# Decay attention with a gated convolution: the turns cut into 64-row halves, the states into column halves, and each copy given an engine of its own

## The chip, the cores and the metric

The kernel runs on one core of a Trainium2 chip, as one launch. The metric is the device time of that core in microseconds (us); lower is better. TensorE (PE in the profile) multiplies, VectorE (DVE) and ScalarE (ACT) work element by element, GpSimd (POOL) copies and issues some transfers, SyncE (SP) issues the other transfers. Results of PE land in PSUM, eight banks, from where DVE or ACT must copy them into SBUF before PE can use them again.

## What is computed

All data are 32-bit floats. For each of 4 batches and 8 heads (768 steps, 48 wide) a complex state of 48 x 48 decays by a per-step factor and takes in an outer product:

```
scale = min(|a|, 0.999) / (|a| + 1e-6);  a = (a_re + i a_im) * scale
S = a[t] * S + outer(k[t], v[t])          # S complex, k and v real
y[t] = q[t] @ real(S)
```

Then y is laid out as x (batch, 768, 384) and goes through a gated layer:

```
gate = sigmoid(sum over 5 taps of conv_w[tap] * x shifted by the tap)
out  = (gate * (x @ w_val)) @ w_out
```

## The kernel before

**The attention.** The products of the decays are written as exp and cos/sin of running sums, so that a head's step t has a key row `kx` and a query row `qx` of 96 numbers (cosine and sine part). The work is cut into nine units (a batch, its heads, a half of its steps; the first unit has two heads, the second six, the other seven eight). For each unit ACT computes logarithms, arctangent, sines and exponentials, DVE the products and running sums between them (`p_ln` to `p_query`, letters a to r of the order), and DVE ends with `kx` and then `qx` (L477).

**Turns.** `kx` and `qx` have steps on the partitions; scores need them with the 96 numbers on the partitions. `flips` (letter T, L526) turns them on PE: three multiplications by the identity per head and half, 128 steps each, into one PSUM bank (`mm`, four of them). `flip_copies` (U) copies the bank into `kT` or `qT`.

**Scores, states, outputs.** Per chunk of 128 steps and pair of heads: `scores` (s, L555 to L560) multiplies kT by qT, in four pieces that lie in the upper or lower 64 partitions of a bank; `masks` (M, L571) multiplies the bank by the causal mask on DVE; `states` (t, L593) adds kn^T v of a chunk to the running state, 96 rows high, in the bank `S_ps`; `state_copies` (u) copies it into `S_sb` or `S_cr`; `outputs` (y, L628 to L638) adds the state's part and the chunk's own part; `output_copies` (v) copies the result into `y_sb`. A multiplication of 32-bit numbers leaves two records of the profile, a turn one. `kn` is `kx` with other steps on the partitions: it is stored to DRAM (`store_kd`, K) and loaded back (`load_kn`, N).

**The layer.** `collects` (X) moves `y_sb` into `xT` by transfers on POOL's queue. `conv` (C and D) runs five taps per 128 channels, the first as a scaled copy on ACT (L147), the other four on DVE (L691). `gates` (G) is the sigmoid on ACT, `values` (P, L722) and `projects` (O, L729) the two multiplications, `gateds` (Z, L746) the product with the gate on DVE, `row_copies` (Q) and `stores` (W) the way out.

**Order.** Every step is a letter, and the string `ORDER` lists all steps once. Instructions are emitted in that order, and `turn` pins each engine's instructions, and SP's and POOL's transfers, to the order of emission. So each engine has one fixed queue, and an instruction that waits holds everything behind it on its engine. Copies out of PSUM are all made by `act_copy` (L149), on ACT.

Of the kernel before, what the change touches and what calls it, by code (L numbers as in the profile page):

```python
# [25 lines left out]
BUFS = {'in': 4, 'v': 2, 'kn': 2, 'xT': 2, 'z': 2, 'lv': 2, 'an': 2, 'tmp': 2, 'qx': 2, 'kx': 1, 'kT': 6, 'S': 1, 'S_sb': 3, 'S_cr': 4, 'y_sb': 3, 'sm': 2, 'ot': 2, 'mm': 4, 'y': 1}  # L26
# [3 lines left out]
TAP0 = 'act'  # L30
ORDER = (
    "AAVLaaAbcceafgadiibclmhhdcwjwwwhhjwkknpewpBfkkwwoVgqArowqriinooTTBAaAaUAlmpbUpTUqATUrKcdqTUTLwssANtr"
    "TaTTuAhMMyhacUjwUUbsvceyvkcMskseBfnKtugfMigTdiyvtuilwooilshympAAANtmvMuTThqUUqtujUUtuprMTrUTTtyTuVUU"
    "UTTTvysMpkUtvTpsMkUsTautaUyuAbUMTvTKUAqUAcywTTvyNcUUsesUMMsrvTntfXXyoouwvgUTMdTtyUUXvTTiUXutqBUAhATr"
    "AhiATwauyUwLUalmpjtsskTTpTvMMbUUsUywcMvkTTcUUwTUyvTXTunTewyUTTqUsTUUwvosoMsyrMwMXvXKNtuATTUfUyvqgBUX"
    "UrPituTXCDDTTtyUUKUuNasMstTTaUiulvDsUyCmXCMTCMtCvCCDPputypGZCUDACvuPtdhTTuhtUTUTCGybUUssjutPvkwXMysk"
    "wPGcuZZZdhtTMMnovoyTUTTZAAqOcrvyqhQXeUTTUTUTUTXXUTUUUTjvUsfAAsrMyaMsvkayMPukvyVOnboBvgcWZKUoNiilmXXX"
    "DXtDuTDCCCOUtQDWTTTDQTAAutUTUUUssDDUcOMWDDupTpMOOrtQTWQTyCCqGWUvsAQDuydMvTUUtuUTTTAAtUqKrhPhGGPyeaUU"
    "sTvjNaZTUMyfubZcgBkPPPkZviiltZXZVmssMydnooTAXpTMTutvyBchqWUTUTUTUTeUUUUTTTUfqOKsspMgMiivysvyhutQUUTr"
    "TTvUMTUlmuAyUUvssMyMrvpsMyvTTjUTTpUUUXXNtuXXkkTTTUtUunPZotuTTqTyBUUUssMMTToTvysvyqUUArrKNUUtuTUTTtuO"  # L40
    "vQXMyUUsvsMyMvsMyvTTtuTTUUUtuUTTtUTTTutUyUUssUXvCDMyvMsyCXCCuvTUMTTCCUUTUtWWPTTTUCyuCUUssXMMvyvCDDDD"
    "CsMyEPvOOQQXWWXOQWGZXXPPPGZGZZZPtODCOOuCDDDDDCCQWDDDDCZQWQWyGvXOQWPZGEEGOQWOQWOCQPPZDCZOOCCCGDQDDDWG"
    "QWXCCPZPPCCCGOZZOOOQWQWWQQWW"
# [9 lines left out]
def kernel(  # L53
# [12 lines left out]
    nc = tc.nc  # L66
# [82 lines left out]
    def act_copy(out, in_):  # L149
        return turn("act", nc.scalar.copy(out, in_))  # L150
# [141 lines left out]
    def weights():  # L292
        cw_row = const.tile([TAPS * NT, P], F32, name="cw_row")
# [91 lines left out]
    def p_sec(u):  # L385
        tf, tj = rate(u, "tmp", "tmp")
        act(tf, views(u, "an")[0], AF.Square)
        yield
        act(tf, tf, AF.Ln, bias=1.0, sets=[LE])
        yield  # L390
# [127 lines left out]
    def flips():  # L518
        for u, (b, h0, g, f0, nf) in enumerate(units):
            for rs, (s, nm) in [(rs, x) for rs in groups[u] for x in ((0, "kx"), (1, "qx"))]:  # L520
                src = tl[u][nm].rearrange("p (j f h) c d -> p j f h (c d)", f=nf, h=g)
                for f in range(nf):
                    for h in [r + w * (g // 2) for r in rs for w in range(2)]:
                        pt = mm().rearrange("p (j x) -> p j x", j=4)
                        for j in range(JH):
                            pe(nc.tensor.transpose(pt[:C2, j, :], src[:, j, f, h, :], ident))  # L526
                        pts.append((u, s, f0 + f, h, pt))
                        yield

    def flip_copies():  # L530
        while True:
            u, s, f, h, pt = pts.pop(0)
            t = sb.tile([C2, HS], F32, name=("kT", "qT")[s], bufs=BUFS["kT"])
            act_copy(t.rearrange("c (p j) -> c p j", j=JH), pt[:C2, :JH].rearrange("c j p -> c p j"))
            tl[u]["T", s, f, h] = t
            yield
# [44 lines left out]
    def states():  # L581
        for i, (u, n, rs) in enumerate(chunks):
            b, h0, g, f0, nf = units[u]
            if n == NCH - 1:
                continue
            if i == firsts[bank(u, rs)]:
                S_ps[bank(u, rs)] = ps.tile([P, 512], F32, name="S_ps", bufs=BUFS["S"])
            kn = tl[u]["kn", n // HN]
            for r in rs:
                for w in range(2):  # L590
                    h = r + w * (g // 2)
                    at = ((n % HN) * g + h) * C2
                    pe(nc.tensor.matmul(  # L593
                        S_ps[bank(u, rs)][:C2, (2 * (h0 + r) + w) * D:(2 * (h0 + r) + w + 1) * D], kn[:, at:at + C2],
                        v_b[b][:, head(u, h), n],
                        start=(i == firsts[bank(u, rs)] and r == rs[0] and w == 0), stop=(n == NCH - 2),
                        skip_group_check=True,
                    ))
            yield

    def state_copies():
        for u, n, rs in chunks:
# [5 lines left out]
            act_copy(t, S_ps[bank(u, rs)][:C2, 2 * (h0 + rs[0]) * D:2 * (h0 + rs[-1] + 1) * D])  # L608
# [74 lines left out]
    def conv(xT, t0, n, c, z):  # L683
        x0, w0 = xT[:, c, EXT + t0:EXT + t0 + n], cw_sb[:, TAPS - 1, c:c + 1]
        if TAP0 == "act":
            act(z, x0, AF.Copy, scale=w0)
        else:
            dve(nc.vector.tensor_scalar_mul(z, x0, w0))
# [11 lines left out]
    def convs(side):  # L700
        for b, t0, n, c in cspans[side::2]:
# [4 lines left out]
            yield from conv(xTs[b], t0, n, c, zs[b, t0][:, c])  # L706
# [118 lines left out]
    def step_by_step():  # L825
# [7 lines left out]
        with ExitStack() as es:  # L833
# [13 lines left out]
            with tc.For_i(0, S, TB) as t0:  # L847
                tl = {}
                for nm, src in (("ar", a_re), ("ai", a_im), ("k", k), ("q", q), ("v", v)):
# [56 lines left out]
                for b in range(B):  # L906
                    nc.sync.dma_start(
                        out=xd[b, ds(t0, TB), :].rearrange("t (h e) -> h t e", e=D), in_=yo[b * H:(b + 1) * H]
                    )
            with tc.For_i(0, B, 1) as b:  # L910
                xn = sp.tile([P, J, DM], F32, name="xn")
                nc.sync.dma_start(out=xn, in_=xd[ds(b, 1)].rearrange("o (p j) c -> (o p) j c", j=J))
# [13 lines left out]
                for t0 in (0, HS):  # L926
# [5 lines left out]
                    for m in range(t0, t0 + HS, P):  # L932
# [4 lines left out]
                        nc.sync.dma_start(out=out[ds(b, 1), m:m + P].rearrange("o p c -> (o p) c"), in_=ot)  # L937
# [32 lines left out]
```

## Time and profile before

| what | value |
|---|---|
| median of 3 runs | 320.6 us (316.15 to 323.51) |
| the profiled execution, its own time | 317.13 us |
| its span, first to last instruction | 315.4 us |
| PE busy | 275.7 us, 87% |
| DVE busy | 240.7 us, 76% |
| ACT busy | 239.1 us, 76% |
| POOL busy | 63.4 us, 20% |
| granted TensorE clock, mean | 0.982 |

The busy time of PE is the union of its modelled intervals: records of multiplications overlap, so the distance from one start to the next tells what one costs, not its own length. DVE and ACT work on one instruction at a time, and their busy time is work. The 40 slices of the page show where each engine is full: a 9 means at least 90%.

### The profile page before, as it was taken

Reading aid. Unit: us, or ns where it says so; the run is one execution under the profiler, and the core shown is the slowest. Engines: PE = TensorE matmul, PEld = TensorE weight load, DVE = VectorE, ACT = ScalarE, POOL = GpSimd, SP = SyncE. Lnnn points to the kernel's source line nnn. Section 1 sums busy time; section 2 is a strip of 40 time slices with the busy share of each in tenths; the row PEclk is TensorE's granted clock in tenths of the full one; section 3 lists DMA queues with packets and bytes.
Section 4 is the critical chain, followed back from the end, with each engine's and each line's share of the span. In section 5 each row is a group of like instructions: output and inputs, shape, how many; then the busy total and the mean of one; then the engine's idle time right before and its main releaser. Section 6 shows DMA issues by size and latency. Waiting matters only on the chain.

```text
span 315.4 us, 7175 instructions
## 1 busy us (share of the span) xinstructions
PE 275.7 (87%) x2887; PEld 211.5 (67%) x2887; DVE 240.7 (76%) x289; ACT 239.1 (76%) x429; POOL 63.4 (20%) x124
## 2 busy tenths in 40 slices
PE   0342959987899999999999999999998999999992
PEld 0121646876687888787778668898898875655551
DVE  4978989997999999999799996983823692281730
ACT  6999989998899999999999899579445515333211
POOL 6410001132017000643400302331333020030000
PEclk9999987997999999999999999999999999999999
DMA  7999999699579498998269698792582012042111
GB/s 185 197 261 316 331 208 172 216 267 279 147 253 224 181 237 214 194 226 240 57 191 271 238 211 146 239 231 60 188 189 72 22 38 77 0 137 76 52 48 58
DMA packets 73748, 54.80 MB, mean 174 GB/s; under 512 B 28511, under 2 KB 70766, under 8 KB 72814
## 3 DMA queue, kind: packets, MB, share of 16 engines
q1 hardware_dynamic: 71150, 49.57, 62.1%
q0 software_dynamic: 2560, 4.72, 6.2%
q8 instruction: 24, 0.39, 0.5%
q14 instruction: 14, 0.11, 0.1%
HBM read 35.40 MB, written 14.16 MB: 157 GB/s over the span
## 4 chain that ended last, share of the span: by engine, by line
PE 58%; ACT 17%; DVE 10%; DMA 9%; issue 2%; SPq 1%; POOL 0%; DVEq 0%; ACTq 0%; POOLq 0%
PE mm L722 14%; PE mm L729 14%; PE mm L526 8%; PE S_ps L593 5%; DMA kn<-kd 5%; PE y_ps L628 4%; DMA kd<-kx 3%; PE sc_ps L555 3%; DVE kx L477 3%; ACT tmp L147 3%; ACT L145 3%; ACT qx L147 2%; PE y_ps L633 2%; PE y_ps L638 2%; ACT lv L147 2%
## 5 line engine op out<-in xcount | busy, mean ns | idle before, releaser
L157 POOL DMA_DIRECT2D xT<-y_sb x80 | 40.3, 510 | 148.3 <-ACT y_sb L150 115.6
L691 DVE SCALAR_TENSOR_TENSOR z<-xT,cw_sb,z 128x768 f32<-128x768 f32 (+1 forms) x60 | 50.4, 862 | 8.3 <-ACT z L147 6.7
L722 PE MATMUL mm<-xT,w_sb 128*128 128x384 f32 x144 | 49.9, 493 | 0.0
L729 PE MATMUL mm<-w_sb,z 128*128 128x384 f32 x144 | 49.2, 491 | 0.0
L571 DVE TENSOR_TENSOR sm<-sc_ps,mask 128x384 f32<-128x384 f32 (+1 forms) x51 | 26.5, 527 | 19.4 <-PE sc_ps L560 16.7
L593 PEld LDWEIGHTS S_ps<-v_in,kn 128*96 128x96 f32 x320 | 33.3, 170 | 9.9 <-issue 5.3
L593 PE MATMUL S_ps<-v_in,kn 128*96 128x48 f32 x320 | 35.1, 251 | 4.2 <-DMA kn<-kd 3.2
L729 PEld LDWEIGHTS mm<-w_sb,z 128*128 128x128 f32 x144 | 26.6, 190 | 16.8
L722 PEld LDWEIGHTS mm<-xT,w_sb 128*128 128x128 f32 x144 | 26.5, 190 | 16.6
L526 PE MATMUL mm<-ident,kx 128*96 128x128 f32 x192 | 30.3, 293 | 8.0 <-DVE kx L477 8.0
L556 PE MATMUL sc_ps<-qT,kT 96*64 96x128 f32 x192 | 37.0, 289 | 0.0
L555 PE MATMUL sc_ps<-qT,kT 96*64 96x128 f32 x192 | 36.5, 287 | 0.5 <-DVE sm L571 0.5
L150 ACT COPY qT<-mm 96x384 f32<-96x384 f32 x64 | 27.8, 494 | 5.4 <-PE y_ps L628 3.0
L145 ACT ACT_TABLE_LOAD x24 | 30.8, 1283 | 1.2 <-PEq L954 0.8
L150 ACT COPY y_sb<-y_ps 112x256 f32<-112x256 f32 (+1 forms) x51 | 18.7, 367 | 16.0 <-PE y_ps L638 15.8
L526 PEld LDWEIGHTS mm<-ident,kx 128*96 128x96 f32 x192 | 21.7, 136 | 11.3 <-issue 9.1
L150 ACT COPY kT<-mm 96x384 f32<-96x384 f32 x64 | 28.8, 487 | 0.3
L526 PE MATMUL mm<-ident,qx 128*96 128x128 f32 x192 | 28.0, 285 | 0.5 <-DVE lv L443 0.5
L557 PE MATMUL sc_ps<-qT,kT 96*64 96x64 f32 x192 | 27.5, 226 | 0.0
L150 ACT COPY ot<-mm 128x384 f32<-128x384 f32 x24 | 11.1, 475 | 21.6 <-PE mm L729 14.6
L560 PE MATMUL sc_ps<-qT,kT 96*64 96x64 f32 x192 | 27.4, 225 | 0.0
L746 DVE TENSOR_TENSOR z<-mm,z 128x384 f32<-128x384 f32 x24 | 13.0, 551 | 18.2 <-PE mm L722 12.0
(90 smaller groups left out, 590.9 us busy)
## 6 DMA issues: line engine op xcount, KB each, us to landing
kd<-kx SPq DMA_DIRECT2D x7, 1152.0 KB, 5.2
out_dram<-ot SPq DMA_DIRECT2D x24, 192.0 KB, 1.9
ar_in<-in_a_re_dram SPq DMA_DIRECT2D x7, 576.0 KB, 7.5
ai_in<-in_a_im_dram SPq DMA_DIRECT2D x7, 576.0 KB, 6.8
k_in<-in_k_dram SPq DMA_DIRECT2D x7, 576.0 KB, 8.4
q_in<-in_q_dram SPq DMA_DIRECT2D x7, 576.0 KB, 9.1
kn<-kd SPq DMA_DIRECT2D x7, 576.0 KB, 4.5
kn<-kd SPq DMA_DIRECT2D x14, 288.0 KB, 6.2
```

Source lines behind the costliest of these rows:

```text
L145: turn("act", nc.scalar.preload_act_table_set(sets[0]))
L150: return turn("act", nc.scalar.copy(out, in_))
L157: ins = (nc.gpsimd if pool else nc.sync).dma_start(**kw)
L526: pe(nc.tensor.transpose(pt[:C2, j, :], src[:, j, f, h, :], ident))
L555: pe(nc.tensor.matmul(lo[:, :C], part(u, 0, ha, n, 0, HC), part(u, 1, ha, n), start=True, stop=True))
L556: pe(nc.tensor.matmul(hi[:, 0::2], part(u, 0, hb, n, 0, HC), qb, start=True, stop=True))
L557: pe(nc.tensor.matmul(lo[:, C:], part(u, 0, hb, n, HC, C), part(u, 1, hb, n, HC, C), start=True, stop=True))
L560: pe(nc.tensor.matmul(hi[:, 1], part(u, 0, ha, n, HC, C), part(u, 1, ha, n, HC, C), start=True, stop=True))
L593: pe(nc.tensor.matmul(S_ps[bank(u, rs)][:C2, (2 * (h0 + r) + w) * D:(2 * (h0 + r) + w + 1) * D], kn[:, at:at + C2], v_b[b][:, head(u, h), ...
L691: dve(nc.vector.scalar_tensor_tensor(out=z, in0=xT[:, c, EXT + t0 - t:EXT + t0 - t + n], scalar=cw_sb[:, TAPS - 1 - t, c:c + 1], in1=z, op ...
L722: pe(nc.tensor.matmul(pv[:, :n], wv_sb[:, ci, c * P:(c + 1) * P], xT[:, ci, EXT + t0:EXT + t0 + n], start=(ci == 0), stop=(ci == NT - 1),))
L729: pe(nc.tensor.matmul(po[:, :DM], z[:, ci, m:m + P], wo_sb[:, ci, :], start=(ci == 0), stop=(ci == NT - 1)))
```

## The change

Five things change together.

- **Turns in 64-row halves.** `flips` now takes a pair of heads in one step. Each block of 128 steps is turned as two blocks of 64 steps (rows 0 to 63 and rows 64 to 127 of the array), and the two halves go to two banks. There are 768 turns of 64 columns where 384 of 128 were. `flip_copies` makes two copies per pair, each of 384 columns, so the copies stay 128 in number and the same in size. The tiles kT and qT hold a pair each, and there are 3 of each instead of 6.
- **States in column halves.** The 96 columns of `kn` are taken as two blocks of 64 (the second runs over into the next head's columns, and their results, rows 96 to 127, are not used). There are 320 such multiplications where 160 of 96 columns were. `kn` is 32 columns longer, and POOL sets those to zero, nine times.
- **Homes.** A table `HOMES` says for each copy out of PSUM, each square and each first tap whether DVE (D) or ACT (A) does it. DVE takes 23 of the 128 turn copies, 11 of the 43 state copies, 12 of the 51 output copies, 6 of the 24 row copies, one of the 9 squares and 8 of the 15 first taps.
- **Order.** The whole string is another one. ACT loads its tables 28 times instead of 24.
- `cw_row` shares a buffer, and the fallback path that isn't run here (`step_by_step`) issues its transfers from POOL's queue.

```
-BUFS = {..., 'kT': 6, ...}
+BUFS = {..., 'kT': 3, ...}
+HOMES = {
+    "v": "DAAADDAAAAADAAAAAAAAAAAAAADAADAADAAAAAAAADADAADAAADD",
+    "Q": "AAAAAAAAAADAADADDDAAAADA",
+    "u": "DDADAAAAAAAAAAAAAAAAAAAAAAAAADDADDDADAAADAD",
...
+    "c": "ADAAAAAAA",
+    "tap": "ADAAADADDADDDDA",
+}
 ORDER = (
-    "AAVLaaAbcceafgadiibclmhhdcwjwwwhhjwkknpewpBfkkwwoVgqArowqriinooTTBAaAaUAlmpbUpTUqATUrKcdqTUTLwssANtr"
...
+    "aabAAcaAceabcVfgiddhhjhilLcVhBkjmkepknpfooknoogAwiilqBAwAwqAwmpKTrAraaATwUUqqUsbTprrUsTcNtwceMMUUUKy"
...
-    def act_copy(out, in_):
+    def copy(key, out, in_):
+        if on_dve(key):
+            return dve(nc.vector.tensor_copy(out=out, in_=in_))
         return turn("act", nc.scalar.copy(out, in_))
...
+        flat = tl[u]["kn", f] = sb.tile([C, HN * g * C2 + C - C2], F32, name="kn", bufs=BUFS["kn"])
+        pool(nc.gpsimd.memset(flat[:, HN * g * C2:], 0.0))
...
-                    for h in [r + w * (g // 2) for r in rs for w in range(2)]:
-                        pt = mm().rearrange("p (j x) -> p j x", j=4)
-                        for j in range(JH):
-                            pe(nc.tensor.transpose(pt[:C2, j, :], src[:, j, f, h, :], ident))
+                    for r in rs:
+                        pt = [mm()[:C2, :2 * JH * HC].rearrange("c (w j p) -> c w j p", w=2, j=JH) for _ in range(2)]
+                        for w in range(2):
+                            for j in range(JH):
+                                for o in range(2):
+                                    at = slice(o * HC, (o + 1) * HC)
+                                    pe(nc.tensor.transpose(
+                                        pt[o][:, w, j, :], src[at, j, f, r + w * (g // 2), :], ident[at, at]
+                                    ))
...
+                    for lo in (0, HC):
+                        pe(nc.tensor.matmul(
+                            S_ps[bank(u, rs)][lo:lo + HC, (2 * (h0 + r) + w) * D:(2 * (h0 + r) + w + 1) * D],
+                            kn[:, at + lo:at + lo + HC], v_b[b][:, head(u, h), n],
...
-        if TAP0 == "act":
+        if on_dve:
+            dve(nc.vector.tensor_scalar_mul(z, x0, w0))
+        else:
             act(z, x0, AF.Copy, scale=w0)
```

Three places of the queues, as they stand before and now (a row is an instruction with its line, its operation, what it writes and reads and the size of the first; x6 is six in a row; the name of a tile is followed by its number).

PE, in the last unit, at the turns of `kx` and `qx` (`mm<-ident`) between states (`S_ps`) and outputs (`y_ps`). Before:

```order
L526 MATMUL mm<-ident,kx 96x128 x6
L593 MATMUL S_ps<-v_in,kn 96x48 x4
L526 MATMUL mm<-ident,kx 96x128 x6
L593 MATMUL S_ps<-v_in,kn 96x48 x4
L526 MATMUL mm<-ident,qx 96x128 x6
L593 MATMUL S_ps<-v_in,kn 96x48 x4
L526 MATMUL mm<-ident,qx 96x128 x6
L526 MATMUL mm<-ident,kx 96x128 x3
L593 MATMUL S_ps<-v_in,kn 96x48 x4
L628 MATMUL y_ps_106<-qT,S_sb 48x128 x4
L633 MATMUL y_ps_106<-sm,v_in 48x64 x4
```

Now, in the same unit:

```order
L624 MATMUL S_ps<-v_in,kn 64x48 x8
L548 MATMUL mm<-ident,kx 96x64 x24
L659 MATMUL y_ps_106<-qT,S_sb 48x128 x4
L664 MATMUL y_ps_106<-sm,v_in 48x64 x4
L669 MATMUL y_ps_106<-sm,v_lo_103 48x64 x4
L624 MATMUL S_ps<-v_in,kn 64x48 x8
L548 MATMUL mm<-ident,qx 96x64 x24
L659 MATMUL y_ps_106<-qT,S_sb 48x128 x4
L664 MATMUL y_ps_106<-sm,v_in 48x64 x4
```

Blocks of six turns (x6, two heads) with a state step behind each became one block of 24 half turns (two pairs of heads, 12 each), and a state step of four multiplications became one of eight; output steps now stand between the blocks.

DVE, up to the last `kx` and just past it. Before:

```order
L571 TENSOR_TENSOR sm<-sc_ps_107,mask 128x384
L430 SCALAR_TENSOR_TENSOR an<-an,mm 128x1152
L435 TENSOR_SCALAR an<-an 128x1152
L746 TENSOR_TENSOR z<-mm,z 128x384
L473 TENSOR_TENSOR em<-em,k_in 128x1152
L571 TENSOR_TENSOR sm<-sc_ps_108,mask 128x384
L571 TENSOR_TENSOR sm<-sc_ps_107,mask 128x384
L477 TENSOR_TENSOR kx<-qx,em 128x2304
L473 TENSOR_TENSOR lv<-lv,q_in 128x1152
L477 TENSOR_TENSOR qx<-qx,lv 128x2304
L571 TENSOR_TENSOR sm<-sc_ps_108,mask 128x384
```

Now:

```order
L163 COPY kT<-mm 96x2x192
L163 COPY S_sb<-S_ps 96x192
L163 COPY kT<-mm 96x2x192
L462 TENSOR_TENSOR lv<-lv,mm 128x1152
L163 COPY y_sb<-y_ps_106 112x2x128
L163 COPY S_sb<-S_ps 96x192
L601 TENSOR_TENSOR sm<-sc_ps_108,mask 128x384
L163 COPY qT<-mm 96x2x192 x3
L601 TENSOR_TENSOR sm<-sc_ps_107,mask 128x384
L163 COPY qT<-mm 96x2x192
L492 TENSOR_TENSOR em<-em,k_in 128x1152
L496 TENSOR_TENSOR kx<-qx,em 128x2304
```

Eight copies out of PSUM (L163) came in ahead of the last `kx` in this stretch. Ahead of the last `kx` in the whole queue there are 260 instructions where 225 were: 17 turn copies, 8 state copies, 8 output copies, two first taps, two masks and one square more, and three products with the gate fewer.

POOL, at the transfers of the last batch but one into `xT`. Before:

```order
L198 COPY v_lo_103<-v_in 64x576 x2
L157 DMA xT<-y_sb 32x384
L157 DMA xT<-y_sb 16x384
L157 DMA xT<-y_sb 48x384 x3
L665 MEMSET xT 128x3x4
L157 DMA xT<-y_sb 48x384 x3
```

Now:

```order
L212 COPY v_lo_103<-v_in 64x576 x2
L171 DMA xT<-y_sb 48x384
L171 DMA xT<-y_sb 16x384
L171 DMA xT<-y_sb 32x384
L222 MEMSET kn 128x32
L171 DMA xT<-y_sb 32x384
L171 DMA xT<-y_sb 16x384
```

Setting 32 columns of `kn` to zero stands between transfers that wait for `y_sb`; the queue runs in this order, so it waits with them, and the states that read those columns wait for it.

## Rows read from the trace of the kernel before

**Rows 1.** The page: busy time, share and instructions; PE in 40 slices.

```profile
PE 275.7 (87%) x2887; PEld 211.5 (67%) x2887; DVE 240.7 (76%) x289; ACT 239.1 (76%) x429; POOL 63.4 (20%) x124
...
PE   0342959987899999999999999999998999999992
```

**Rows 2.** Stretches: length; busy us of PE, PEld, DVE, ACT, POOL; clock; DMA share; GB/s.

```profile
0.00:97.00 97.00, 64.89 (x694) 51.08 (x694) 84.63 (x105) 90.22 (x154) 19.30 (x43) 0.95 0.96 238
97.00:190.00 93.00, 92.54 (x1026) 71.47 (x1025) 89.79 (x97) 89.10 (x146) 23.52 (x41) 1.00 0.83 204
190.00:223.80 33.80, 33.62 (x508) 29.57 (x505) 24.45 (x26) 26.51 (x58) 10.61 (x20) 1.00 0.68 160
223.80:315.40 91.60, 84.63 (x673) 59.42 (x671) 41.78 (x65) 33.27 (x75) 10.00 (x21) 0.99 0.26 80
```

**Rows 3.** The chain of waits from the last kx on: start, length, engine.

```profile
221.23 2.57 DVE kx L477
223.81 5.63 DMA kd<-kx
...
237.47 0.68 PE S_ps L593 x6
...
292.12 3.87 PE mm L729 x12
...
309.61 0.48 ACT ot L150
```

**Rows 4.** PE in order of time: start, length, line, records merged.

```profile
105.29 0.80 PE L593 MATMUL S_ps<-v_in,kn 128*96 128x48 f32 x8
105.93 0.82 PE L526 MATMUL mm<-ident,qx 128*96 128x128 f32 x6
106.59 0.50 PE L526 MATMUL mm<-ident,kx 128*96 128x128 f32 x3
106.93 0.80 PE L593 MATMUL S_ps<-v_in,kn 128*96 128x48 f32 x8
107.66 0.65 PE L628 MATMUL y_ps<-qT,S_sb 96*48 96x128 f32 x8
...
108.58 0.28 PE L555 MATMUL sc_ps<-qT,kT 96*64 96x128 f32 x1
108.59 0.28 PE L556 MATMUL sc_ps<-qT,kT 96*64 96x128 f32 x1
108.69 0.27 PE L555 MATMUL sc_ps<-qT,kT 96*64 96x128 f32 x1
...
108.80 0.22 PE L557 MATMUL sc_ps<-qT,kT 96*64 96x64 f32 x1
108.81 0.22 PE L560 MATMUL sc_ps<-qT,kT 96*64 96x64 f32 x1
108.86 0.22 PE L557 MATMUL sc_ps<-qT,kT 96*64 96x64 f32 x1
```

**Rows 5.** Turns (L526), then states (L593), by stretch: length, busy PE and PEld, clock.

```profile
97.00:223.80 126.80, 26.91 (x201) 20.97 (x199) 1.00 0.79 192
223.80:315.40 91.60, 7.47 (x57) 6.16 (x57) 0.99 0.26 80
...
97.00:223.80 126.80, 18.35 (x179) 17.90 (x180) 1.00 0.79 192
223.80:315.40 91.60, 6.43 (x64) 6.06 (x62) 0.99 0.26 80
```

**Rows 6.** Groups of DVE and ACT instructions by form: busy us, mean ns.

```profile
L571 DVE TENSOR_TENSOR sm<-sc_ps,mask 128x384 f32<-128x384 f32 x45 | 24.5, 551 | 19.4 <-PE sc_ps L560 16.7 <-PE y_ps L638 1.8
L571 DVE TENSOR_TENSOR sm<-sc_ps,mask 128x192 f32<-128x192 f32 x6 | 2.0, 348 | 0.0
L435 DVE TENSOR_SCALAR an<-an 128x1152 uint32<-128x1152 uint32 x7 | 5.3, 763 | 0.1
L150 ACT COPY kT<-mm 96x384 f32<-96x384 f32 x64 | 28.8, 487 | 0.3
L145 ACT ACT_TABLE_LOAD x24 | 30.8, 1283 | 1.2 <-PEq L954 0.8
```

More of the change, by code (lines that the diff above doesn't have):

```diff
@@ L147, in act, with on_dve @@
         return turn("act", nc.scalar.activation(*args, **kw))
-    def act_copy(out, in_):
+    homes = {key: list(at) for key, at in HOMES.items()}
+    def on_dve(key):
+        return homes[key].pop(0) == "D"
+    def copy(key, out, in_):
+        if on_dve(key):
+            return dve(nc.vector.tensor_copy(out=out, in_=in_))
         return turn("act", nc.scalar.copy(out, in_))
@@ L386, in p_sec @@
         tf, tj = rate(u, "tmp", "tmp")
-        act(tf, views(u, "an")[0], AF.Square)
+        tan = views(u, "an")[0]
+        if on_dve("c"):
+            dve(nc.vector.tensor_tensor(out=tf, in0=tan, in1=tan, op=ALU.mult))
+        else:
+            act(tf, tan, AF.Square)
         yield
@@ L531, in flip_copies @@
         while True:
[L532 to L536, printed above, removed]
+            u, s, f, r, pt = pts.pop(0)
+            b, h0, g, f0, nf = units[u]
+            t = sb.tile([C2, 2, HS], F32, name=("kT", "qT")[s], bufs=BUFS["kT"])
+            for w in range(2):
+                tl[u]["T", s, f, r + w * (g // 2)] = t[:, w]
+            for o in range(2):
+                copy(
+                    "U", t[:, :, o * HS // 2:(o + 1) * HS // 2].rearrange("c w (p j) -> c w p j", j=JH),
+                    pt[o].rearrange("c w j p -> c w p j"),
+                )
+                yield
     def part(u, s, h, n, lo=0, hi=C):
@@ L592, in states @@
                     at = ((n % HN) * g + h) * C2
[L593 to L598, printed above, removed]
+                    for lo in (0, HC):
+                        pe(nc.tensor.matmul(
+                            S_ps[bank(u, rs)][lo:lo + HC, (2 * (h0 + r) + w) * D:(2 * (h0 + r) + w + 1) * D],
+                            kn[:, at + lo:at + lo + HC], v_b[b][:, head(u, h), n],
+                            start=(i == firsts[bank(u, rs)] and r == rs[0] and w == 0), stop=(n == NCH - 2),
+                            skip_group_check=True,
+                        ))
             yield
@@ L607, in state_copies @@
             t = sb.tile([C2, 2 * len(rs) * D], F32, name=nm, bufs=BUFS[nm])
[L608 removed]
+            copy("u", t, S_ps[bank(u, rs)][:C2, 2 * (h0 + rs[0]) * D:2 * (h0 + rs[-1] + 1) * D])
             for r in rs:
@@ L700, in convs @@
     def convs(side):
-        for b, t0, n, c in cspans[side::2]:
+        for (b, t0, n, c), home in list(zip(cspans, HOMES["tap"]))[side::2]:
             if (b, t0) not in zs:
@@ L705, in convs @@
                 )
-            yield from conv(xTs[b], t0, n, c, zs[b, t0][:, c])
+            yield from conv(xTs[b], t0, n, c, zs[b, t0][:, c], home == "D")
     def gates():
@@ L758, in row_copies @@
             ot = sb.tile([P, DM], F32, name="ot", bufs=BUFS["ot"])
-            act_copy(ot, pos.pop(0)[:, :DM])
+            copy("Q", ot, pos.pop(0)[:, :DM])
             ots.append(ot)
```

51 lines of the change are left out of this document (25 added, 26 removed).

## The prediction

> **What bounds the kernel now.** First the page: PE is busy for 87% of the span, DVE and ACT for 76% each, and PE's slices are full from the twelfth on but for one and the last [rows 1]. A mean over such a span misleads, so next come the stretches [rows 2]. Up to 97 us ACT is the fullest (90.2 of 97) and PE has much to wait for. From 97 to 190 all three are full: PE 92.5 of 93, DVE 89.8, ACT 89.1. From 190 on DVE and ACT thin out and PE stays full, 33.6 of 33.8 and then 84.6 of 91.6. The chain of waits ties the last two together [rows 3]: the last `kx` leaves DVE at 223.8, its way through DRAM takes until 237.5, under other work of PE, and from 223.8 on PE is in one dense piece to 309.6, where the last row copy begins. So the span is a sum of four:
>
> DVE's work up to the last `kx` (84.6 + 89.8 + 24.5 = 198.9) + DVE's idle time till then (24.9) + PE's stretch behind it (309.6 - 223.8 = 85.8) + the last copy, its store and the end (5.8) = 315.4.
>
> PE's own unit prices are distances between starts, since its records overlap [rows 4]. Six turns of 128 columns take 105.93 to 106.59: 0.110 us each. Eight records of states take 0.64: 0.080 each. Where the engine's shape changes next (states to outputs) the same eight take 106.93 to 107.66, 0.73, so a change costs 0.09. Twelve records of a projection take 3.87 [rows 3]: 0.3225 each, 0.645 for a multiplication.
>
> **The turns.** A turn becomes two halves, 64 rows each. Whether two halves overlap no row shows, since no instruction here uses half of the rows. The nearest is two instructions in different column halves: L555 and L556 start 0.01 apart, and the next L555 comes 0.11 behind the first; with 64 columns (L557, L560) the pair takes 0.06 [rows 4]. So pairs do overlap in the columns, and time follows the columns streamed. Bounds for a pair of half turns: 0.055 (as L557 with L560) and 0.16 (no overlap, each the 0.080 that 96 columns of states take). I take 0.055, the row nearest in size. Then 384 x (0.110 - 0.055) = 21 us of PE's work goes, 201 turns of them between 97 and 223.8 and 57 behind [rows 5]: 11 and 3 us.
>
> The Trainium skill, "TensorE: Matmul & The Clock Gate", section "Part 4: PE-mode transpose", gives about 275 ns for a turn inside a kernel, 173 ns of it an access latency that halving would not shorten. By it (an estimate from that page) 384 turns would be 106 us now and 768 half turns over 170 us, and the change would lose some 60. The rows disagree: 0.110 from start to start, with the latency under the neighbours.
>
> **The states.** 320 records at 0.080 become 320 pairs with 64 columns of weights. L557 with L560 have the same 64 columns: 0.055 for a pair. The bounds are 0.055 and 0.11 (no overlap). I take 0.055: 179 records between 97 and 223.8 give 4.5 us, 64 behind give 1.6 [rows 5].
>
> **Changes of shape.** By the order PE goes from whole rows and columns to halves and back 88 times before, 126 times now, as turns have a shape of their own. 38 x 0.09 = 3.4 us more, 25 of them in the middle stretch, five behind the last `kx`.
>
> So PE has some 13 us less to do (11 + 4.5 - 2.3) in a stretch of 127 in which it was full. It stops being the limit there, and DVE is late next.
>
> **DVE.** It gets 61 pieces. A price comes from the two masks out of PSUM: 0.551 us for 384 columns, 0.348 for 192 [rows 6], a line of 0.145 us and 1.06 ns a column. The lower bound is L435, 0.763 for 1152, or 0.66 ns a column. I take the line, since PSUM is the source; first taps read SBUF, and I give them 0.76. Ahead of the last `kx` the order puts 17 turn copies (9.4), 5 + 3 state copies (1.7 + 0.7), 5 + 3 output copies (2.1 + 0.8), two taps (1.5), a square (1.1), two masks more and three products fewer (-0.5): 16.8 us. So 215.7 of work in place of 198.9; at the lower bound 4 us less.
>
> **ACT.** It gives away 23 turn copies at 0.487, 11.2 us, and 38 other pieces, and gets four table loads at 1.283, 5.1 us [rows 6]. It is no fuller than before at any point, and DVE is ahead of it from the last third on: ACT's saving is worth what DVE can use, and no more.
>
> **DVE's idle time.** Before, 12.4 up to 97 us (ACT 6.8), then 3.2 in 93 (3.4%), then 9.4 in 33.8, where masks and products waited for PE (L571 waited 16.7 us for PE's scores in all) [rows 2, 6]. Now the two engines share the early load more evenly: I let DVE have done 87.4 by 97 us, midway between the two. Of the rest, 128.3, idle time lies between none and the 3.4% seen with three full engines; with PE relieved I take half, 1.75%: 130.6 us. The last `kx` is then done at 227.6, not 223.8. The bounds: 90.2 done by 97 and no idle time, 222.5; 84.6 and 3.4%, 232.8. The copies' lower price takes 4 off.
>
> **PE behind the last `kx`.** By the order: 57 turns become 48 pairs (6.3 to 2.6), 64 records of states become 56 pairs (5.1 to 3.1), three multiplications of values more (+1.9), six of projections fewer (-3.9), outputs and scores a tenth fewer (-1.3), five changes of shape (+0.5): 85.8 - 8.5 = 77.3.
>
> Setting `kn`'s last columns to zero costs POOL little, and I cost it at nothing: POOL is busy for 20% [rows 1], and the loads of the same `kn` wait for the same buffer. If that cover goes, it is a rival below. The halved number of kT tiles holds as many heads as before.
>
> **The sum.** 227.6 + 77.3 + 5.8 = 310.7 us of span, with the 1.7 around it 312.4, against 317.1 for the profiled execution: 1.5% less. The bounds give 307 to 318 (303 with cheap copies). The profiled execution is 1.1% under the median of the three runs, 320.6; the same share off the median is 315.9. I say 314, between the two.
>
> **Rivals.**
>
> 1. *The order fills better than I allow.* For it: ACT kept 96% with PE full all the time, and PE now has slack. With both lower bounds, 218.5 for the last `kx`, and 2 us of PE's work done ahead of it, the span is 300 and the time 301, or 305 at the median's level. Against it: DVE had those 12.4 us of early idle time from a start that is still a chain of ACT and DVE. Chance 0.15; faster.
> 2. *Half turns don't overlap (slower).* Row halves are shown by nothing here. If each half turn takes 0.055 and follows the other, turns save nothing; if the column halves of states don't either, 243 records cost 0.03 more each, 7 us; with 30 changes of shape, 2.7, PE is full again from 97 on and is 10 us longer: 327. At 0.080 a half it is 258 x 0.05 = 13 us more, 340. It decides from a pair of about 0.10 us on, where PE has no slack beside DVE. Against it are the column pairs [rows 4]. A fixed part of each turn, as the Trainium skill's page "TensorE: Matmul & The Clock Gate" has it, would end in this case too. Chance 0.12.
> 3. *A state step waits for POOL.* The nine settings of `kn` stand in a queue among transfers that wait for `y_sb`. PE's states wait for them, and with them all behind. A delay shows only where PE or DVE have no other work; at two or three places of 2.5 us each it gives 318 to 322, no change. Against it: SP's load of `kn`, 13.7 us from the last `kx` to its states [rows 3], is the longer way. Chance 0.08.
> 4. *My forecast*, DVE setting the pace up to the last `kx` and PE behind it. Chance 0.65, of which 0.27 lie beyond 2% and 0.38 within it, since 1.5% is close to the line.
>
> Two per cent is about what a measurement of this kernel can tell from no change. Faster by over 2%: 0.27 + 0.15 = 0.42. Within 2%: 0.38, 0.06 of the third rival and 0.01 of the second: 0.45. Slower: 0.11 + 0.02 = 0.13. For the range, the forecast's bounds at the median's level and the first rival give the low end, 304; the high end, 323, leaves out most of the second.
>
> **What would show it.** Right: pairs of half turns start within 0.01 to 0.02 and follow each other by 0.055 to 0.06; state pairs likewise; DVE busy for 266 to 270 us and fuller than PE between 97 and 225; the last `kx` ending at 223 to 233; PE dense behind it for 76 to 79 us. Wrong: starts of half turns 0.05 or more apart one by one; idle time of PE ahead of states that POOL ends; DVE's copies at 0.3 us instead of 0.55; or a granted clock below 1.00 behind 97 us, where it was 1.00 before [rows 2], since a less busy PE could lose it in the stretch that sets the end.

## The result, and the profile after the change

The changed kernel takes 307.07 us (median of four: three at 305.46 to 307.56, the fourth at 345.30) beside 319.93 us for the kernel before on the same chip: a ratio of 0.962, 95% interval 0.950 to 0.974. All ratios here leave out executions over 1.5% above the shortest of the same kernel, as that fourth one is; the profiled executions of two kernels of the table below (rows apart with whole states, and all on ACT) are over it too, so their rows are upper bounds. The change is faster by 3.8%; forecast was 1.5 to 2%. The profiled execution took 307.56 us, its span is 306.0, that is 9.4 less than the 315.4 before.

The page of the changed kernel (as [rows 1]): busy time, share and instructions; PE in 40 slices.

```profile
PE 255.8 (84%) x3591; PEld 191.2 (62%) x3591; DVE 262.2 (86%) x350; ACT 222.0 (73%) x372; POOL 67.9 (22%) x133
...
PE   0224855869977987998979999999999999999995
```

PE is busy for 20 us less and DVE for 21.5 more. Some of PE's slices are under nine up to the twenty-first; before they were full from the twelfth on but for one and the last. Its stretches, with the columns of [rows 2], cut at the end of the last `kx`, which is now at 223.72 (221.16 and 2.56 long):

```profile
0.00:97.00 97.00, 59.10 (x963) 47.64 (x964) 89.66 (x118) 91.72 (x148) 20.55 (x45) 0.93 0.99 250
97.00:190.00 93.00, 84.85 (x1433) 65.86 (x1428) 88.51 (x105) 85.09 (x144) 29.55 (x53) 0.96 0.88 215
190.00:223.72 33.72, 33.71 (x483) 25.32 (x484) 31.31 (x39) 24.35 (x39) 7.34 (x14) 1.00 0.36 107
223.72:306.00 82.28, 78.17 (x722) 52.40 (x720) 52.70 (x92) 20.84 (x43) 10.42 (x22) 1.00 0.27 85
```

In the middle stretch PE is busy for 84.9 of 93 us, not for 92.5, and in the last it is dense again. The chain of waits shows what it does there, and where it ends (start, length, engine; as [rows 3]):

```profile
228.18 0.45 PE S_ps L624 x16
228.63 0.81 PE mm L548 x24
229.44 0.60 PE S_ps L624 x16
...
296.60 5.82 PE mm L760 x18
302.48 0.48 ACT ot L164
```

Twelve pairs of half turns (24 records) take 0.81 us with the changes of shape before and behind them. Eight pairs of state halves take 0.45 behind scores, which have their shape, and 0.60 behind turns, which have not. The last row copy starts at 302.48. So the four terms of the forecast can be read off, and the same for each kernel run later (times in us from the profiled execution; the clock is the granted TensorE clock up to the last `kx`, a mean of its two levels, 1.00 for 2.4 GHz and 0.50 for 1.2; the ratio is to the kernel before on the same chip):

| kernel | span | last `kx` ends | DVE busy, idle till then | PE busy till then | clock till then | PE's stretch behind | end | ratio, 95% interval |
|---|---|---|---|---|---|---|---|---|
| before | 315.4 | 223.8 | 198.9, 24.9 | 191.0 | 0.98 | 85.8 | 5.8 | 1 |
| forecast | 310.7 | 227.6 | 215.7, 11.9 | | | 77.3 | 5.8 | 0.985 |
| changed | 306.0 | 223.7 | 209.5, 14.2 | 177.7 | 0.95 | 78.8 | 3.5 | 0.962, 0.950 to 0.974 |
| changed, second look | 302.0 | 220.5 | 209.1, 11.5 | 178.3 | 0.95 | 78.0 | 3.5 | 0.956, 0.951 to 0.960 |
| row halves apart | 306.2 | 222.6 | 209.8, 12.8 | 183.4 | 0.95 | 80.2 | 3.4 | 0.959, 0.948 to 0.970 |
| whole states | 312.1 | 227.6 | 210.5, 17.0 | 189.6 | 0.94 | 81.1 | 3.5 | 0.978, 0.968 to 0.989 |
| turns twice | 319.1 | 233.1 | 209.8, 23.3 | 192.5 | 0.96 | 82.5 | 3.5 | 1.010, 1.004 to 1.017 |
| rows apart, whole states | 317.4 | 232.3 | 210.8, 21.5 | 195.3 | 0.93 | 81.7 | 3.4 | 0.983, 0.966 to 1.001 |
| all on ACT | 329.5 | 243.0 | 197.6, 45.5 | 188.7 | 0.91 | 82.9 | 3.7 | 1.022, 1.009 to 1.035 |
| before, state halves | 315.3 | 222.1 | 198.2, 24.0 | 186.1 | 0.98 | 87.4 | 5.7 | 0.996, 0.989 to 1.004 |
| before, table of homes | 332.8 | 234.4 | 208.4, 26.0 | 196.5 | 0.94 | 92.7 | 5.7 | 1.046, 1.036 to 1.055 |
| before, fallback on POOL | 314.3 | 224.0 | 198.5, 25.5 | 189.1 | 0.98 | 86.7 | 3.6 | 0.986, 0.979 to 0.992 |
| changed, fallback on SP | 305.6 | 221.9 | 209.4, 12.4 | 174.3 | 0.97 | 78.0 | 5.7 | 0.962, 0.955 to 0.969 |
| the same, second run | 306.9 | 222.9 | 209.6, 13.4 | 177.4 | 0.95 | 78.2 | 5.7 | 0.965, 0.960 to 0.971 |

The same instructions keep PE busy for longer at a lower clock, so PE's column holds both; rows with the same clock compare its work.

From before to changed, 7.1 of the 9.4 us come from PE's stretch behind the last `kx`, 2.3 from the end, and nothing from the last `kx` itself (3.3 us in the second look): DVE does 10.6 us more by then and idles 10.7 less. Where that idle time was is shown by DVE's waits up to the last `kx` (who it waits for: us in total, times, longest). The longest for PE before:

```profile
DVE z L746 <- PE mm L722: 3.2, 1, 3.2
DVE lv L443 <- PE mm L363: 3.1, 3, 1.5
DVE sm L571 <- PE sc_ps L560: 2.5, 3, 1.6
```

And in the changed kernel:

```profile
DVE an L449 <- PE mm L378: 1.4, 2, 1.0
DVE sm L601 <- PE sc_ps L590: 0.8, 2, 0.7
```

All of them for PE together went from 14.0 to 4.8 us (2.3 in the second look): 9.2 of the 10.7. The masks alone show less than [rows 6] suggests: of the 19.4 us that they waited before, 14.6 lie behind the last `kx`, where DVE does not set the pace. The same groups of the changed kernel (busy us, mean ns of one, idle time before them and who ended it):

```profile
L601 DVE TENSOR_TENSOR sm<-sc_ps,mask 128x384 f32<-128x384 f32 x45 | 24.4, 549 | 1.7 <-PE sc_ps L590 1.6
L163 DVE COPY kT<-mm 96x384 f32<-96x384 f32 x12 | 6.3, 544 | 0.9 <-PE mm L548 0.7
L163 DVE COPY y_sb<-y_ps 112x256 f32<-112x256 f32 x9 | 3.7, 416 | 1.0 <-PE y_ps L669 1.0
```

The masks wait 1.7 us in all, and the copies that came to DVE hardly wait either: PE is ahead of DVE now. The copies last what the forecast's line gave them (0.544 and 0.416 against 0.551 and 0.416).

### The profile page after: what moved, and what is told of

Read it like the earlier page. It is cut to its first block, busy times and chain, and to the rows that moved or that the text cites. A ratio compares the mean times of both kernels' runs of the same rounds, so it can differ in the third digit from the quotient of the medians.

```text
span 306.0 us, 8620 instructions
## 1 busy us (share of the span) xinstructions
PE 255.8 (84%) x3591; PEld 191.2 (62%) x3591; DVE 262.2 (86%) x350; ACT 222.0 (73%) x372; POOL 67.9 (22%) x133
## 4 chain that ended last, share of the span: by engine, by line
PE 52%; DVE 21%; ACT 14%; issue 5%; DMA 5%; POOL 2%; SPq 0%; DVEq 0%; ACTq 0%; POOLq 0%
PE mm L760 14%; PE mm L753 14%; PE mm L548 4%; PE y_ps L659 4%; PE S_ps L624 3%; PE sc_ps L585 3%; PE mm L378 3%; DVE z L722 3%; PE y_ps L664 2%; ACT lv L154 2%; PE y_ps L669 2%; ACT an L154 2%; ACT L152 2%; DVE lv L462 2%; DMA xT<-y_sb 2%
## 5 line engine op out<-in xcount | busy, mean ns | idle before, releaser
L722 DVE SCALAR_TENSOR_TENSOR z<-xT,cw_sb,z 128x768 f32<-128x768 f32 (+1 forms) x60 | 51.9, 875 | 6.1 <-ACT z L154 3.1
L585 PE MATMUL sc_ps<-qT,kT 96*64 96x128 f32 x192 | 37.6, 293 | 3.8 <-ACT qT L164 3.6
L586 PE MATMUL sc_ps<-qT,kT 96*64 96x128 f32 x192 | 37.6, 293 | 0.0
L164 ACT COPY ot<-mm 128x384 f32<-128x384 f32 x18 | 8.5, 475 | 35.1 <-PE mm L760 31.1
L624 PE MATMUL S_ps<-v_in,kn 128*64 128x48 f32 x640 | 28.3, 230 | 5.3 <-ACT S_cr L164 4.3
L624 PEld LDWEIGHTS S_ps<-v_in,kn 128*64 128x64 f32 x640 | 24.1, 145 | 9.4 <-ACT S_cr L164 4.5
L212 POOL COPY v_lo<-v_in 64x576 f32<-64x576 f32 (+2 forms) x18 | 20.6, 1147 | 40.9 <-PE y_ps L669 25.3
L164 ACT COPY qT<-mm 96x384 f32<-96x384 f32 x53 | 23.4, 487 | 3.9 <-PE y_ps L659 1.9
L587 PEld LDWEIGHTS sc_ps<-qT,kT 96*64 96x64 f32 x192 | 25.3, 145 | 1.2 <-issue 1.2
L590 PEld LDWEIGHTS sc_ps<-qT,kT 96*64 96x64 f32 x192 | 25.2, 145 | 0.4 <-issue 0.4
L164 ACT COPY kT<-mm 96x384 f32<-96x384 f32 x52 | 23.1, 484 | 2.2 <-PE mm L548 1.9
L664 PE MATMUL y_ps<-sm,v_in 128*48 128x64 f32 x384 | 21.2, 229 | 3.2 <-ACT y_sb L164 2.1
L585 PEld LDWEIGHTS sc_ps<-qT,kT 96*64 96x64 f32 x192 | 19.7, 144 | 6.7 <-ACT qT L164 4.1
```

What stands on the lines that cost most here:

```text
L585: pe(nc.tensor.matmul(lo[:, :C], part(u, 0, ha, n, 0, HC), part(u, 1, ha, n), start=True, stop=True))
L586: pe(nc.tensor.matmul(hi[:, 0::2], part(u, 0, hb, n, 0, HC), qb, start=True, stop=True))
L587: pe(nc.tensor.matmul(lo[:, C:], part(u, 0, hb, n, HC, C), part(u, 1, hb, n, HC, C), start=True, stop=True))
L590: pe(nc.tensor.matmul(hi[:, 1], part(u, 0, ha, n, HC, C), part(u, 1, ha, n, HC, C), start=True, stop=True))
L624: pe(nc.tensor.matmul(S_ps[bank(u, rs)][lo:lo + HC, (2 * (h0 + r) + w) * D:(2 * (h0 + r) + w + 1) * D], kn[:, at + lo:at + lo + HC], v_b[b ...
L664: pe(nc.tensor.matmul(to(r, w, HC, C), v_b[b][:, head(u, h), n], sm[:, r, (1 + w) * HC:(2 + w) * HC], start=(n == 0 and r == 0), stop=Fals ...
```

## The experiments

Three theories. **A:** PE's saving in the turns and states makes the gain; new order and homes only turn it into time. **B:** order and homes make it, and PE's saving ahead of the last `kx` is not needed. (The texts written ahead of two runs use A and B for other things; it is said there.) **C**, beside either: 2 us of it come from the fallback path, which isn't run, but whose transfers moved from SP's queue to POOL's.

### Row halves apart

```
-for w in range(2):
-    for j in range(JH):
-        for o in range(2):
-            at = slice(o * HC, (o + 1) * HC)
+for o in range(2):
+    at = slice(o * HC, (o + 1) * HC)
+    for w in range(2):
+        for j in range(JH):
```

> The changed kernel with one thing else: within a step the six half turns of rows 0 to 63 come first, then the six of rows 64 to 127, so that neighbours use the same row half. Theory A (the two row halves work at the same time, and PE's saving is what keeps it off the path): half turns now follow one by one at 0.05 to 0.06 us, 12 in about 0.65 instead of 0.33; 768 of them are 42 us, 21 more than in the changed kernel. Behind the last kx the 48 pairs cost 2.6 us more; ahead of it PE had about 16 us to spare and takes some 16 us more, in places where it is full: 2 to 6 more there. Time 5 to 9 us over the changed kernel. Theory B (order and homes made the gain; PE's saving ahead of the last kx is not needed): 2 to 3 us over it. Theory C (halves don't depend on neighbours, a half turn costs 0.027 by itself): no change.

Measured 307.6 us, ratio 0.959 (0.948 to 0.970), against 0.956 and 0.962 for the changed kernel: no difference that these runs can tell, where theory A had 5 to 9 us. PE in order of time (start, length, line, records):

```profile
127.79 0.70 PE L548 MATMUL mm<-ident,qx 64*96 64x64 f32 x12
128.42 0.64 PE L659 MATMUL y_ps<-qT,S_sb 96*48 96x128 f32 x8
```

Twelve half turns take 0.63 us to the next instruction, about as expected. What they take in pairs is in the chain of the changed kernel, for blocks of 24 and of 12:

```profile
91.89 0.81 PE mm L548 x24
...
94.40 0.47 PE mm L548 x12
```

Six pairs more take 0.34 us, 0.056 for one, and 0.14 is left for the way into the shape and out. One by one, twelve would take 0.81, if a half turn by itself costs what a pair does. So the edit undid half of the overlap, 0.16 of 0.34 us: the second half's turns begin while the first half's still run. In this block three of the twelve starts lie within 0.006 us of another one; six alternating pairs have six such. PE is busy 5.8 us longer ahead of the last `kx`, and neither the last `kx` (222.6, between the two looks at the changed kernel) nor the time answers. It doesn't decide between A and B. It suggests that PE has some 6 us to spare, as far as single executions can tell: the two looks at the changed kernel lie 3 us apart.

### Whole states

```
-for lo in (0, HC):
-    pe(nc.tensor.matmul(S_ps[bank(u, rs)][lo:lo + HC, ...], kn[:, at + lo:at + lo + HC], ...
+pe(nc.tensor.matmul(S_ps[bank(u, rs)][:C2, ...], kn[:, at:at + C2], ...
```

> The changed kernel with the states taken back: 160 multiplications with 96 columns of weights instead of 320 with 64. Theory A: records follow by 0.080 instead of pairs by 0.058; 320 x 0.022 = 7 us more work of PE, some 1.4 of them behind the last kx, and a bit less in changes of shape. Ahead of it PE's slack hides most: 1.5 to 3.5 us over the changed kernel. Theory B (PE's saving ahead of the last kx is not needed): 1 to 1.5 us. If the columns don't overlap at all: no change or faster.

Measured 313.2 us, ratio 0.978 (0.968 to 0.989): 6 to 9 us over the changed kernel, more than either theory gave. PE between scores and turns:

```profile
232.27 0.22 PE L587 MATMUL sc_ps<-qT,kT 96*64 96x64 f32 x1
232.28 0.22 PE L590 MATMUL sc_ps<-qT,kT 96*64 96x64 f32 x1
232.43 0.88 PE L623 MATMUL S_ps<-v_in,kn 128*96 128x48 f32 x8
233.24 0.88 PE L548 MATMUL mm<-ident,kx 64*96 64x64 f32 x24
```

And the same place in the changed kernel:

```profile
227.95 0.22 PE L587 MATMUL sc_ps<-qT,kT 96*64 96x64 f32 x1
227.96 0.22 PE L590 MATMUL sc_ps<-qT,kT 96*64 96x64 f32 x1
228.01 0.62 PE L624 MATMUL S_ps<-v_in,kn 128*64 128x48 f32 x16
228.56 0.88 PE L548 MATMUL mm<-ident,kx 64*96 64x64 f32 x24
```

The step itself takes 0.81 instead of 0.55. But it also starts 0.15 behind the last score instead of 0.05: whole states have another shape than the scores and outputs beside them, state halves have the same. By the order the changed kernel has 126 changes of shape, with whole states 168. Together PE is busy 11.9 us longer ahead of the last `kx` and 2.8 behind it, twice the 7 expected; some 3 us of it at most can be the clock's, 0.94 in place of 0.95. The last `kx` comes 4 us later (7 against the second look). Theory A, with a term, the changes of shape, that I had not priced.

### Both together

> The changed kernel with both savings of PE taken away (half turns one by one, states with 96 columns): the new order and the homes alone. Theory A: PE has 28 us more, 4 behind the last kx, 20 ahead of it where 16 are to spare but not everywhere; the last kx comes 5 to 12 us later; time 9 to 16 us over the changed kernel, about the kernel before or above it, PE full from 97 us on again. Theory B: 4 us over it, still some 8 us under the kernel before.

Measured 317.8 us, ratio 0.983 (0.966 to 1.001), its edit being the last two at once. Order and homes without state halves, and with half of the row halves' overlap, are thus worth 2%, give or take 2, and some 2 us of that is the shorter end (below). B, which had 8 us under the kernel before, is not excluded by the ratio alone.

### Turns twice

To undo all of the turns' saving, each half turn is done twice, so that one pair of heads costs what two did:

```
-for o in range(2):
+for o in (0, 1, 0, 1):
     at = slice(o * HC, (o + 1) * HC)
```

> The changed kernel with each half turn done twice in a row (the second writes the same values): 1,536 half turns, whose 768 pairs at 0.052 to 0.056 cost PE what 384 whole turns at 0.109 cost, so turns save nothing any more, and all else is as in the changed kernel. Behind the last kx 48 pairs more: 2.6 us. Ahead of it PE has 15 us more. Theory A (PE has some 6 us to spare there, as the row halves apart showed, and from there on each us of PE's counts): the last kx 6 to 9 us later, time 8 to 12 us over the changed kernel. Theory B (PE's saving ahead of the last kx is not needed): 2.6 to 4 us over it.

Measured 321.7 us beside 304.4 for the changed kernel on the same chip: 17.3 more, ratio 1.010 (1.004 to 1.017). That is theory A, at one and a half times its size: with order, homes and state halves in place but turns as dear as before, nothing of the gain is left. The clock is no rival here, 0.96 up to the last `kx` beside 0.95. The twelve pairs of a head pair's step now take the 0.81 us of two head pairs before. PE has 14.8 us more ahead of the last `kx`, which comes 9 us later than in the first look and 12.5 later than in the second; the stretch behind grows by 4. DVE waits for PE again up to the last `kx`, 13.8 us where it was 4.8, which is nearly the whole delay; the two longest:

```profile
DVE sm L601 <- PE sc_ps L590: 4.5, 6, 1.3
DVE z L777 <- PE mm L753: 2.5, 1, 2.5
```

So the time seems to answer little to the first 6 us of PE's work and then almost fully, each point being one execution: PE busy for 178, 183, 190 and 192.5 us ahead of the last `kx` puts it at 220.5 to 223.7, 222.6, 227.6 and 233.1, with DVE's own work at 209 to 211 in all of them. The sum of PE's busy time isn't the whole of it: with both together PE is busy for 195 and the last `kx` comes no later than with turns twice. Some 5 us of these 195 can be the clock's, 0.93 beside 0.96; whether it also counts where in the order the work stands was not followed up.

### All on ACT

```
 def on_dve(key):
-    return homes[key].pop(0) == "D"
+    return False
...
-            yield from conv(xTs[b], t0, n, c, zs[b, t0][:, c], home == "D")
+            yield from conv(xTs[b], t0, n, c, zs[b, t0][:, c], False)
```

> The changed kernel with all 61 pieces of the table HOMES on ACT: the halves and the order alone. Ahead of the last kx ACT gets 17 turn copies (8.3 us), 16 state and output copies (some 5), two taps and a square (3), so 205 of 223.7 us of work become 221 or more; DVE has 17 less. Theory A (ACT and DVE set the pace ahead of the last kx, and neither had 17 us to spare): the last kx 8 to 17 us later, behind it ACT has time enough, 1 to 3 us more; time 9 to 20 us over the changed kernel. Theory B (PE's relief alone made the gain): no more than 3 us over it.

Theories A and B of this text are not those above: A has ACT and DVE set the pace, B has PE's relief alone make the gain.

Measured 327.8 us, ratio 1.022 (1.009 to 1.035): 21 to 23 us over the changed kernel, past the 20 that this A allowed, and this B is refuted. From 0.00 to the end of the last `kx`:

```profile
0.00:243.03 243.03, 188.68 (x2866) 148.16 (x2867) 197.56 (x224) 213.23 (x365) 56.30 (x111) 0.91 0.79 197
```

ACT gets 12 us more and DVE 12 less, and the last `kx` comes 19 us later, DVE idling for 45. The masks wait 13.3 us for scores up to there (0.8 in the changed kernel), though PE has slack: in the whole run PE waits 6.0 us for turns, 8.5 for states and 5.8 for outputs that ACT has not copied yet, where it was 3.6, 4.3 and 2.9. ACT had no room for them: without the homes the order, with all halves, is slower than the kernel before. Part of the loss can be the clock's. It was at 0.91 where it had been 0.95, and PE is busy for 11 us longer with the same instructions; whether it fell because PE waited, or PE came late because it fell, no run separates.

### State halves alone, and homes alone, in the kernel before

```
-        flat = tl[u]["kn", f] = sb.tile([C, HN * g * C2], F32, name="kn", bufs=BUFS["kn"])
+        flat = tl[u]["kn", f] = sb.tile([C, HN * g * C2 + C - C2], F32, name="kn", bufs=BUFS["kn"])
+        pool(nc.gpsimd.memset(flat[:, HN * g * C2:], 0.0))
...
+                    for lo in (0, HC):
```

> The kernel before with the states in column halves alone (kn 32 columns longer and set to zero there by POOL). PE, full from 97 us on, has 320 x 0.022 = 7 us less, 1.4 of them behind the last kx. Theory A (PE sets the pace between 97 and 224 together with DVE and ACT): 2 to 5 us under the kernel before. Theory B (DVE and ACT set it, PE merely looks full): 1 to 1.5 us under it. If setting kn to zero holds states up: no gain, or slower.

Here A has PE set the pace together with DVE and ACT, B has DVE and ACT set it alone.

Measured 319.7 us, ratio 0.996 (0.989 to 1.004): no gain that these runs can tell. At most it is 3.6 us, which leaves this B and the lower part of this A. PE is busy 4.9 us less ahead of the last `kx` and as long behind it. Here states stand beside whole turns, and where states had their shape, state halves don't: 136 changes by the order where the kernel before has 88. PE behind the last `kx`:

```profile
231.02 0.86 PE L527 MATMUL mm<-ident,kx 128*96 128x128 f32 x6
231.81 0.67 PE L595 MATMUL S_ps<-v_in,kn 128*64 128x48 f32 x16
232.42 0.86 PE L527 MATMUL mm<-ident,kx 128*96 128x128 f32 x6
```

Six turns and a state step take 1.40 us here, from 231.02 to 232.42. In [rows 4], without a change between them, they took 1.30 (0.64 for the states and 0.66 for the turns): at such a place the halves cost more than they save.

The table of homes alone, in the kernel before, with its order and whole turns (each `act_copy`, square and first tap asks the table, as in the changed kernel):

> The kernel before (its own order, whole turns, states of 96 columns) with the table of homes alone: DVE takes 61 of the copies, squares and first taps, by the changed kernel's table. Theory A (with PE full from 97 on, neither engine's relief is worth much, and DVE has more to do ahead of the last kx): between 3 us under and 8 us over the kernel before. Theory B (homes alone make a good part of the gain): 4 us or more under it.

Measured 334.4 us, ratio 1.046 (1.036 to 1.055), beyond all that was expected, and against B: DVE does 9.5 us more ahead of the last `kx` and doesn't idle less, since PE is late for it there. Here too the clock can have a part: 0.94 up to the last `kx` where it was 0.98, with PE busy for 5.4 us longer on the same instructions, and 0.57 from 238 to 246 us, in the stretch behind, which is 7 us longer. In the old order the table costs more than it gives. Alone, homes lose and state halves gain nothing that these runs can tell; halves and order without homes lose; together the three gain. The order alone and the half turns alone were not run.

### The fallback path's queue

The same edit both ways: in `step_by_step` all four `nc.sync.dma_start` of the kernel before become `nc.gpsimd.dma_start`, and back in the changed kernel.

> The kernel before with one thing else: the transfers of the fallback path, which isn't run, are issued from POOL's queue instead of SP's. Theory C (SP stands at the end until its instructions behind the skipped path are there, from 310.5 to 313.2, and then counts semaphores): the part behind the last copy is 3.5 us instead of 5.8, time 2.0 to 2.5 us under the kernel before. Rival (the end is set by the last store alone): no change.

Measured 318.3 us beside 320.1 in medians, ratio 0.986 (0.979 to 0.992); the end, from the start of the last copy, is 3.6 us instead of 5.8. The 1.8 us of the medians fit the end; the ratio says twice as much, and the end gives no reason for more.

> The changed kernel with the transfers of the fallback path back on SP's queue. Theory C: the part behind the last copy is 5.8 us again instead of 3.5, time 2.0 to 2.5 us over the changed kernel. Rival: no change.

Measured 307.05 us, as the changed kernel on another chip: the end was 5.7 again, but the last copy started 2.6 us earlier. So both went once more, side by side.

> The changed kernel as it is, on the same chip as the next two, to compare them with: 306 to 308 us, 0.96 to 0.97 of the kernel before. All theories alike.

> The changed kernel with the fallback path's transfers back on SP's queue, a second time, beside the changed kernel on one chip. Theory C (SP stands 2.2 us longer behind the last copy, as the traces of both kernels before and after have it): 2 to 2.5 us over the changed kernel. Rival (something ahead of the last copy gives it back, as the 2.6 us earlier last copy of the first such trace would have it): the same time as the changed kernel, with the last copy 2 us earlier again.

Measured 304.4 us for the changed kernel (303.6 to 305.3, 2 us under what was expected) and 307.2 with the path on SP (306.3 to 310.7): 2.8 us more, ratios 0.956 (0.951 to 0.960) and 0.965 (0.960 to 0.971). What SP waits for in the last 11 us with the path on SP (waiting engine and line, who it waits for, us in total, times, longest):

```profile
SPq L171 <- ACT ot L164: 6.4, 1, 6.4
SPq L970 <- SPq L970: 2.6, 1, 2.6
SPq L171 <- ACTq L970: 1.8, 1, 1.8
```

And in the kernel before, from 305 on:

```profile
SPq L157 <- ACT ot L150: 4.6, 3, 1.9
SPq L939 <- SPq L939: 2.7, 1, 2.7
```

SP waits 2.6 to 2.7 us for itself at the branch past the fallback path (L970, L939). The changed kernel has no such row. Theory C holds in all thirteen traces of the table, 5.7 to 5.8 us at the end with the path on SP and 3.4 to 3.7 with it on POOL, and in both comparisons on one chip. That the wait is for SP's own next instructions is argued: from the row naming SP alone, and from the transfers in that wait, one of which is of instructions (path on SP, second run, 302.1 to 304.6 us: packets, MB, share of 16 engines):

```profile
q14 instruction: 1, 0.01, 1.0%
```

Which engine's instructions it brings, the trace does not say. In the changed kernel SP goes on 0.5 us behind the branch (303.4 to 303.9), and no such transfer runs in between. The Trainium skill, "Runtime: NRT & Kernel Launch", section "Instruction fetch mechanics", says that a branch taken out of the window of loaded instructions stalls until its target has been fetched; the rows would fit, and the page gives no time for it.

No version tried beats the changed kernel.

## Why the prediction was right, and where its size was off

The sum of four terms was the right account, and the table shows its terms moving as the edits move them. Forecast and measured span are 310.7 and 306.0: DVE's work was put 6.2 us too high and the end 2.3, DVE's idle time 2.3 too low and PE's stretch behind the last `kx` 1.5. The gain is twice the forecast's, and the forecast had held a change within 2% (0.45) as likely as a larger one (0.42); 2.3 us of the gain come by a way that it did not have.

- **Half turns and state halves.** Right: 0.055 was taken for a pair of each; six more pairs of turns take 0.34 us, eight pairs of states 0.45, so 0.056 for both. The second rival is refuted. The 275 ns for a turn (the Trainium skill, "TensorE: Matmul & The Clock Gate", "Part 4: PE-mode transpose") is no price in a row of turns: whole ones follow by 0.110 us in [rows 4], pairs of halves by 0.056.
- **PE behind the last kx.** 77.3 forecast, 78.8 and 78.0 measured. Turns twice and whole states lengthen it by 4 and by 2 to 3, at a clock of 1.00: it is PE's own work.
- **DVE's idle time.** 11.9 forecast, 14.2 and 11.5 measured. The reason was right: PE stopped being late, and DVE's waits for it fell from 14.0 to 4.8 us.
- **DVE's work, the failed step.** 16.8 us more forecast, 10.6 measured. The pieces and nearly all of their lengths were right (a first tap takes 0.61, not 0.76): summed over its records, DVE's work ahead of the last `kx` rose from 211.3 to 226.7, by 15.5. But records overlap, as PE's do:

```profile
62.41 0.55 DVE L601 TENSOR_TENSOR sm<-sc_ps,mask 128x384 f32<-128x384 f32 x1
62.88 0.28 DVE L163 COPY y_sb<-y_ps 112x128 f32<-112x128 f32 x1
63.08 0.55 DVE L601 TENSOR_TENSOR sm<-sc_ps,mask 128x384 f32<-128x384 f32 x1
63.54 1.35 DVE L429 SCALAR_TENSOR_TENSOR lv<-lv,tmp 128x1152 f32<-128x1152 f32 x1
```

Here the next one starts 0.47 us after a start of 0.55, 0.20 after one of 0.28: a piece that follows at once costs its length less 0.08. Before, 155 of DVE's 224 followed so up to the last `kx`, now 215 of 259; the overlap went from 12.4 to 17.3 us. I took distances between starts for PE and lengths for DVE, and said of DVE above that it works on one instruction at a time and that its busy time is work; the union of busy time is, a sum of lengths isn't. With 2.3 us more of idle time than forecast, that put the last `kx` 3.9 us late. The sign that DVE would be busy for 266 to 270 us failed by it too: 262.2.
- **The end, the other failed step.** It was taken as unchanged at 5.8, and the move of the fallback path's transfers, being in code that isn't run, was given no cost. It is worth 2.0 to 2.4 us in the traces of the table.
- **The level.** The kernel before was profiled at 317.1 us, under its medians of 319 to 322; profile to profile the change is 3.0%, in medians 3.8 to 4.5. I took half of that difference into the forecast. Why executions of one kernel spread by 2 to 3 us (the second look at the changed kernel has its last `kx` 3.2 us earlier with equal work) stays open.
- **The first rival**, an order that fills better, had the last `kx` at 218.5; the two looks, 223.7 and 220.5, lie between it and the forecast. Less through idle time, as it had it, than through DVE's work.
- **The third rival**, states waiting for POOL, is not seen: no wait of PE in the changed kernel ends with POOL, and state halves in the kernel before, with the same settings of `kn` to zero, are no slower than it.
- **The clock.** Between 97 and 190 us it was granted at 0.96 on average where it had been 1.00, in two pieces of 3.4 us at 0.50 (1.2 GHz), from 98.9 and 160.4 us, ahead of which PE had been busy for 15.3 of 18.9 and for 8.7 of 10.4 us; the prediction named a clock below 1.00 behind 97 us as a sign of being wrong. From 190 on it is 1.00. In the stretch that sets the end it was not lost.

## What to carry to other kernels

Where three engines go in lock step, relief of one is worth what the two others can fill, and to fill it work must move: halves, homes and order had to come together: homes alone lost, state halves alone gained nothing that could be told, and without the homes the rest lost. Price a piece by the distance between starts on every engine, not by its record. And before halving an instruction for a tiled array, look at the shapes of its neighbours: the saving can lie in the changes of shape that go, or be eaten by those that come.

## What the runs showed of the hardware that was not expected

- Two multiplications of one tiling shape follow each other without a price (scores to state halves 0.05 us), two of different shapes with one (scores to whole states 0.15). The Trainium skill, "TensorEngine Tiling (Array Packing)", section "Key Properties", says that changing the tiling mode drains the engine; the rows agree and price it at some 0.07 to 0.10 us.
- Half turns of one row half, six in a row, still overlap in part with the six of the other that follow them: 0.63 us for twelve, where 0.47 is measured for pairs and 0.81 would be none (an estimate from the pairs).
- Code that is skipped cost some 2.2 us at the end of this program when its transfers stood on SP's queue, and not when they stood on POOL's.
